# Moving one small product of a fused attention and feed-forward kernel ahead of group 6's turns

## The chip, the cores and the metric

The kernel runs on one core of one Trainium2 chip, as a single program. The metric is the device time of that program in microseconds (us). Five engines work side by side and wait for each other through semaphores: PE (matrix products; its weight loads are listed as PEld), DVE and ACT (vector and scalar work), POOL (here small copies and its own DMA queue) and SP (the queue from which most DMAs are issued).

## What is computed

The reference chains three stages on 1536 tokens (2 batches of 768), 8 heads of 64 columns. Cut to what matters here:

```python
k_sum = k.reshape(B, H, nb, 32, D).max(axis=3)      # nb = 24 blocks of 32 keys
v_sum = v.reshape(B, H, nb, 32, D).mean(axis=3)     # the "v means"
scores_l = scale * q @ k.T        # kept where |i - j| < 16
scores_s = scale * q @ k_sum.T + log(32)
a = softmax(concat[scores_l masked, scores_s])
attn = a @ concat[v, v_sum]
h = relu(x @ w_in); x = h * h @ w_out               # first feed-forward stage
out = silu(g) * val @ w_out2                        # second: RMS norm, gate and value products
```

## The kernel before, in words

Attention is done in 12 groups of 128 tokens, six for each batch: groups 0 to 5 are batch 0, groups 6 to 11 batch 1. For each group g the code has these steps, and the names are those of the rows below:

- `scores(g)`: PE writes the scores into two PSUM tiles, `s0` and `s1` (line 495).
- `softmax(g)`: DVE adds the mask (523) and takes the maximum `mx` (535; for some groups 541 and 542, with the subtraction on DVE). ACT takes the exponentials of `t`: eight small ACTIVATEs, one for each head (537), or one large one (543). DVE multiplies by the inverse sums, the norm (547).
- `ptrans(g)`, the group's "turns": PE turns `t` in two halves of four heads into `pps` (557), ACT copies each half to `pT` (560).
- `av(g)`: PE multiplies `pT` by `vx` into `xps` (581). `vx` holds, for each of four half-group slots, 96 rows of v (loaded by four DMAs of SP, line 475, the step `vload`) and the 24 rows of v means.
- `split_xs`: ACT casts `xps` to `xhi` (570), DVE forms the rest `xlo` (571). These are the input of the first feed-forward stage.

The rows of a large feed-forward product are laid between these steps: `h` = x times w_in (620) and `y` = the squared activation `hhi`, `hlo` times w_out (642), in passes of 256 tokens. Pass k needs the xhi and xlo of groups 2k and 2k+1: pass 3 (`h_3_0`, `h_3_2`) needs groups 6 and 7.

The v means of batch 1 are made apart from this. Seven accumulating DMAs of POOL add up `vsum` (409). `vs_mean(1)` multiplies it by a constant matrix into the PSUM tile `vmean` (414) and DVE copies that to `vm` (417). `vmput(0, 4)` lets POOL copy `vm` into the means' rows of all four slots of `vx` (462). av(6) is the first to read them.

Weights come as 64-bit words: SP loads them raw (`raw_wi`, line 188; `raw_wo`, line 192), and ACT and DVE turn them into numbers (203 to 224), in units that the loop slips between the other work.

A scheduler sets the final order on every engine: it takes the steps as the code writes them, plays them with its own estimates of duration, and lays each engine's instructions in the order in which they came out. `with after(...)` pins an instruction behind a marked one. Every engine then runs its list in order. The PSUM tiles of the attention steps are given out in turn from four buffers, in the order in which the code asks for them.

Of the kernel before, what the change touches and what calls it, by code (L numbers as in the profile page):

```python
# [32 lines left out]
def tile_window_attention_moe_moe2(  # L33
# [31 lines left out]
    GPB = S // P  # L65
    NG = NT // P
# [264 lines left out]
    def after(*marks):  # L331
        es = ExitStack()
        for m in marks:
            es.enter_context(tc.issue_after(mark[m].ins))
        return es
# [3 lines left out]
    def psA(name, shape=None):  # L339
        tag = rot["tags"][rot["i"] % len(rot["tags"])]  # L340
        rot["i"] += 1
        pool, bufs = {"a": (psB, 2), "h": (psB, 2), "y": (psY, MT // 2), "x": (psX, 2)}[tag]
        return pool.tile(shape or [P, 512], F32, tag=tag, name=name, bufs=bufs)
# [20 lines left out]
    def prep_begin(b):  # L364
        ksum = ap_.tile([P, NPAIR, NB], F32, tag="ksum", name=f"ksum{b}", bufs=1)
        state[b] = ksum

    def prep_load(b, c):
        state[("k", b, c)] = token_chunk(k, b, c, f"kr{b}_{c}")

    def prep_k(b, c):
        ksum = state[b]
        nb1 = 2 * P // QT
        kr = state.pop(("k", b, c))
        nb2 = 2 * P // BLK
        for hf in range(2):
            ps = psA(f"kps{b}_{c}_{hf}", [P, 2, 2 * P])
            for i in range(2):
                p = 2 * hf + i
                for j in range(2):  # L380
                    nc.tensor.transpose(
                        ps[:, i, j * P : (j + 1) * P], kr[:, j, p * P : (p + 1) * P], ident
                    )
            nc.vector.tensor_reduce(
                ksum[:, 2 * hf : 2 * hf + 2, nb2 * c : nb2 * (c + 1)],
                ps.rearrange("d p (n j) -> d p n j", j=BLK),
                axis=AX.X, op=ALU.max,
            )
            kv = kT[:, 2 * hf : 2 * hf + 2, WIN : WIN + NW1 * STEP].rearrange(
                "d p (n s) -> d p n s", s=STEP  # L390
            )[:, :, nb1 * c : nb1 * (c + 1)]
            pv = ps.rearrange("d p (n s) -> d p n s", s=QT)
            nc.scalar.copy(kv[:, :, :, 0:WIN], pv[:, :, :, 0:WIN])
            nc.scalar.copy(kv[:, :, :, WIN + NB : QT + NB], pv[:, :, :, WIN:QT])
# [11 lines left out]
    def vs_load(b):  # L406
        src = v[b].rearrange("h (p e) d -> p h e d", e=NE)
        for e in range(1, NE):
            mark["vs"] = nc.gpsimd.dma_start(vsum, src[:, :, e, :], accum_op=ALU.add)

    def vs_mean(b):
        ps = psA(f"vmean{b}", [K1, DM])[G0:K1]
        with after(("tr", GPB)):
            nc.tensor.matmul(ps, indv, vsum.rearrange("p h d -> p (h d)"), start=True, stop=True)
        vm = ap_.tile([K1, DM], F32, tag="vm", name=f"vm{b}", bufs=1)[G0:K1]
        state["vm"] = vm
        nc.vector.tensor_copy(vm, ps)
# [40 lines left out]
    def vrows(i0, n):  # L458
        return vx[G0:K1, i0 : i0 + n].rearrange("k i h d -> k i (h d)")

    def vmput(i0, n):
        nc.gpsimd.tensor_copy(vrows(i0, n), state["vm"].unsqueeze(1).to_broadcast([NB, n, DM]))
# [88 lines left out]
    def ptrans(g):  # L551
        t = state.pop(("t", g))
        pT = ap_.tile([NK, H, P], F32, tag="pT", name=f"pT{g}", bufs=2)
        for hf in range(2):
            ps = psA(f"pps{g}_{hf}")
            for j in range(4):
                mark[("tr", g)] = nc.tensor.transpose(  # L557
                    ps[0:NK, j * P : (j + 1) * P], t[:, 4 * hf + j, :], ident
                )
            mark[("pT", g)] = nc.scalar.copy(pT[:, 4 * hf : 4 * hf + 4, :], ps[0:NK].rearrange("n (h s) -> n h s", h=4))  # L560
        state[("pT", g)] = pT
# [11 lines left out]
    def av(g):  # L573
        pT = state.pop(("pT", g))
        ps = psA(f"xps1_{g}")
        for u in range(2):
            for p in range(NPAIR):
                o = p * P + QT * u
                for e in range(2):
                    with after(*((("s", 2),) if g == 1 else ())):  # L580
                        mark[("av", g)] = nc.tensor.matmul(  # L581
                            ps[QT * e : QT * e + QT, o : o + QT],
                            vx[:, (2 * g + u) % NVX, 2 * p + e, :],
                            pT[:, e * NPAIR + p, QT * u : QT * u + QT],
                            start=True, stop=True,
                        )
        split_xs(ps, g, 1)
        state["done"] = g
# [156 lines left out]
    def group(g):  # L745

        scores(g)
        if g > 3:
            vload(g)
        softmax(g)  # L750
        if g + 2 < NG and g % 2 == 0:
            qload(g + 2)
# [82 lines left out]
    def h_pair(k_, f):  # L835
        ps = psB.tile([P, CH], F32, tag="h", name=f"h0_{k_}_{f}", bufs=2)
        m = 2 * k_ % MT
        for j in range(2):
            units1.until(("wi", f + j))
            product(ps[:, G2 * j : G2 * (j + 1)], W[("wi", f + j)], xs[(1, 2 * k_ // MT)], m, m + 2)  # L840
        t = square(ps, f"0_{k_}_{f}")
        hq[(k_, f)] = hsplit(t, CH, f"0_{k_}_{f}")

    def y_pair(k_, f, between=()):
        if f == 0:
            for m in range(2):
                ys[m] = y_tile(k_, m, "y0_")
        hh = hq.pop((k_, f))
        for j in range(2):
            units1.until(("wo", f + j))  # L850
            ff_out(
                [ys[m] for m in range(2)], [t[:, G2 * j : G2 * (j + 1)] for t in hh],
                W[("wo", f + j)], f + j == 0, f + j == ROUNDS1[0] - 1,
            )
            if between:
                between[j]()
        if k_ == NK2 - 1:
            units1.used += 4
        if f == ROUNDS1[0] - 2:
            for m in range(2):  # L860
                gather(2 * k_ + m, ys.pop(m), 0, ROUNDS1, "y", None)
# [3 lines left out]
    for k_ in range(NK2):  # L865
        g, last = 2 * k_ + 3, 2 * k_ + 3 >= NG
        h_pair(k_, 0)
        if k_ == 0:
            av(2)
            group(4)  # L870
        if not last:
            ptrans(g)
        h_pair(k_, 2)
        if not last:
            av(g)
        if g == GPB - 1:
            group(GPB)
        if g + 2 < NG:
            group(g + 2)
            if k_ == 0:  # L880
                for c in range(NC2):
                    prep_load(1, c)
                vs_load(1)
        y_pair(k_, 0)
        if g + 1 < NG:
            ptrans(g + 1)
        if g + 1 == GPB:
            vs_mean(1)
            vmput(0, 4)
        if k_ == 0:  # L890
            prep_begin(1)
            prep_k(1, 0)
            y_pair(k_, 2, (lambda: prep_k(1, 1), lambda: prep_k(1, 2)))
            prep_kend(1, nc.vector, 0, NW1)
        else:
            if g + 3 < NG:
                qprep(g + 3)
            y_pair(k_, 2)
        if g + 1 < NG:
            av(g + 1)  # L900
        if k_ == 0:
            qprep(GPB)
        elif g + 3 < NG:
            group(g + 3)
        if k_ == 2:
            units1.cap = NW - 3
            units1.load(units1.cap)
            units1.lim = len(units1.units)
            units1.behind = (("exp", 9), ("norm", 9))
        if k_ == NK2 - 1:  # L910
            units1.behind = ()
        for _ in range(TICKS[k_]):
            units1.tick()
        if not last and g == NG - 1:
            actx.close()
            rot["tags"] = ("a",)
            side["cb"] = ctx.enter_context(
                tc.tile_pool(name="cbpool", bufs=1, side="right", reuse_waits="tile")
            )
            grow = side["cb"].tile([P, DM], F32, tag="grow", name="grow")  # L920
            side["pool"] = hand.enter_context(
                tc.tile_pool(name="w2pool", bufs=1, side="right", reuse_waits="tile")
            )
            side["psum"] = ctx.enter_context(
                tc.tile_pool(name="psY2", bufs=1, space=PSUM, reuse_waits="tile")
            )
            nc.sync.dma_start(grow, rms_g.partition_broadcast(P))
            units1.cap = NW + NRIGHT - 3
# [292 lines left out]
```

## Time and profile before

| | |
|---|---|
| median of 3 runs | 634.95 us (634.86 to 636.49) |
| the profiled execution | 636.93 us, its span 635.2 us |
| PE busy | 619.2 us, 97% of the span |
| DVE, ACT busy | 475.2 us (75%), 381.2 us (60%) |
| granted clock of PE, mean | 0.995 |

The profile follows one execution. Its times count from the start of the span; the 1.7 us between the span and the execution's time lie around it. Busy times say how full an engine is, the rows of waits say what an engine stood still for, and the timeline says when. The granted clock is 1.00 when PE runs at 2.4 GHz and 0.50 at 1.2 GHz. Group numbers are left out in the trace's rows, so that a row is told from its like by its time.

### The profile page before, as it was taken

The numbers are of one execution on the slowest core, as the hardware profiler recorded it, in microseconds if no ns is written. First come the engines' busy times: TensorE is split into PE (matmuls) and PEld (weight loads), VectorE is DVE, ScalarE is ACT, GpSimd is POOL, SyncE is SP. The second block draws the span as 40 slices with busy tenths as digits, with TensorE's granted clock in tenths as the row PEclk, the third lists the DMA queues.
The fourth block names the chain that finished last, engine by engine and source line by source line (L and its number), as shares of the span: only waits on it lengthen the run. The fifth ranks groups of instructions, "written<-read, shape, count | busy, mean of one in ns | idle before, by whom it ended". The sixth has DMA issues, their size and how long they took to land.

```text
span 635.2 us, 10103 instructions
## 1 busy us (share of the span) xinstructions
PE 619.2 (97%) x3794; PEld 522.5 (82%) x3794; DVE 475.2 (75%) x893; ACT 381.2 (60%) x823; POOL 54.6 (9%) x81
## 2 busy tenths in 40 slices
PE   8988998999999999999999999999999999999997
PEld 6576887888888888888888889889889888898886
DVE  4799776959996279987457869996977968976334
ACT  5795576757673257564443748867757567655252
POOL 4012110000000000000000000003112022022040
PEclk9998998999999999999999999999999999999999
DMA  9999913525333123220000005444734745535054
GB/s 245 287 209 211 179 29 84 179 54 166 99 101 99 34 66 101 71 96 0 1 1 1 2 0 199 134 133 68 173 97 83 179 91 95 147 46 87 1 85 115
DMA packets 85873, 64.23 MB, mean 101 GB/s; under 512 B 51904, under 2 KB 75456, under 8 KB 85824
## 3 DMA queue, kind: packets, MB, share of 16 engines
q1 hardware_dynamic: 74576, 51.72, 27.7%
q0 software_dynamic: 11248, 11.87, 13.0%
q8 instruction: 30, 0.49, 0.3%
q14 instruction: 19, 0.16, 0.1%
HBM read 49.94 MB, written 13.63 MB: 100 GB/s over the span
## 4 chain that ended last, share of the span: by engine, by line
PE 87%; DVE 7%; ACT 2%; DMA 1%; issue 1%; SPq 1%; DVEq 0%
PE y L642 20%; PE h L620 19%; PE z L642 15%; PE qa L1002 10%; PE qc L1002 5%; PE pa L1002 5%; PE pc L1002 3%; PE qb L1002 3%; PE s L495 1%; PE pps L557 1%; PE pb L1002 1%; PE xps L581 1%; PE xps L598 1%; DVE mx L531 1%; DMA kr<-in_k_dram 1%
## 5 line engine op out<-in xcount | busy, mean ns | idle before, releaser
L620 PE MATMUL h<-xhi,w_wi 128*128 128x512 f32 (+1 forms) x480 | 134.8, 354 | 4.6 <-ACT xhi L570 3.0
L642 PE MATMUL y<-w_wo,hhi 128*128 128x512 f32 x384 | 118.0, 393 | 1.6 <-DVE w_wo L224 0.8
L620 PEld LDWEIGHTS h<-xhi,w_wi 128*128 128x128 f32 x480 | 86.8, 194 | 17.9 <-ACT xhi L570 4.2
L620 PE MATMUL h<-xlo,w_wi 128*128 128x512 f32 (+1 forms) x240 | 85.0, 355 | 1.4 <-DVE xlo L571 1.4
L642 PEld LDWEIGHTS y<-w_wo,hhi 128*128 128x128 f32 x384 | 71.1, 188 | 16.8 <-DVE w_wo L224 1.2
L642 PE MATMUL z<-w_wp,hhiz 128*128 128x512 f32 x272 | 79.2, 390 | 0.0
L1037 POOL DMA_DIRECT2D out_dram<-zs x40 | 35.4, 1306 | 490.0 <-ACT zs L1033 490.0
L642 PE MATMUL y<-w_wo,hlo 128*128 128x512 f32 x192 | 72.8, 391 | 0.0
L642 PEld LDWEIGHTS z<-w_wp,hhiz 128*128 128x128 f32 x272 | 50.6, 188 | 10.2
L826 ACT ACTIVATE r<-h 128x512 f32<-128x512 f32 x48 | 28.8, 600 | 41.3 <-PE h L620 41.3
L620 PEld LDWEIGHTS h<-xlo,w_wi 128*128 128x128 f32 x240 | 46.7, 194 | 7.5 <-DVE xlo L571 2.1
L827 DVE TENSOR_TENSOR r<-h,r 128x512 f32<-128x512 f32 x48 | 32.9, 685 | 21.8 <-ACT r L826 21.8
L642 PE MATMUL z<-w_wp,hloz 128*128 128x512 f32 x136 | 48.1, 389 | 0.0
L631 ACT CAST hhi<-r 128x512 fp32r<-128x512 f32 x48 | 29.9, 622 | 25.9 <-DVE r L827 25.8
L642 PEld LDWEIGHTS y<-w_wo,hlo 128*128 128x128 f32 x192 | 35.9, 188 | 7.5 <-issue 0.2
L632 DVE TENSOR_TENSOR hlo<-r,hhi 128x512 fp32r<-128x512 f32 x48 | 33.8, 704 | 10.6 <-ACT hhi L631 10.3
L1033 ACT COPY zs<-z 128x512 f32<-128x512 f32 x48 | 25.6, 592 | 9.9 <-PE z L642 9.3
L642 PEld LDWEIGHTS z<-w_wp,hloz 128*128 128x128 f32 x136 | 25.5, 188 | 5.4
L1121 DVE TENSOR_TENSOR sg<-pb,sg 128x256 f32<-128x256 f32 x12 | 5.0, 423 | 25.3 <-PE pb L1002 25.3
L560 ACT COPY pT<-pps 120x512 f32<-120x512 f32 x24 | 13.9, 612 | 14.9 <-PE pps L557 14.8
L657 DVE TENSOR_TENSOR yp<-y,yp 128x512 f32<-128x512 f32 x24 | 15.6, 682 | 8.4 <-PE y L642 8.4
L537 ACT ACTIVATE t<-t,mx 128x120 f32<-128x120 f32 x48 | 18.3, 383 | 1.2 <-DVE mx L535 1.2
(246 smaller groups left out, 1327.1 us busy)
## 6 DMA issues: line engine op xcount, KB each, us to landing
out_dram<-zs POOLq DMA_DIRECT2D x40, 256.0 KB, 6.7
raw_wi<-in_moe_w_in_dram SPq DMA_DIRECT2D x16, 512.0 KB, 4.8
raw_wo<-in_moe_w_out_dram SPq DMA_DIRECT2D x16, 512.0 KB, 4.5
raw_wg<-in_moe_w_gate_dram SPq DMA_DIRECT2D x12, 512.0 KB, 3.7
raw_wv<-in_moe_w_val_dram SPq DMA_DIRECT2D x12, 512.0 KB, 4.6
raw_wp<-in_moe_w_out_dram SPq DMA_DIRECT2D x12, 512.0 KB, 3.3
kr<-in_k_dram SPq DMA_DIRECT2D x12, 256.0 KB, 4.4
qr<-in_q_dram SPq DMA_DIRECT2D x12, 256.0 KB, 4.7
```

Of the source, the lines that this page charges most:

```text
L537: mark[("exp", g)] = nc.scalar.activation(t[:, h], src[h], AF.Exp, bias=mx[:, h : h + 1], accum_out=sm[:, h : h + 1])
L560: mark[("pT", g)] = nc.scalar.copy(pT[:, 4 * hf : 4 * hf + 4, :], ps[0:NK].rearrange("n (h s) -> n h s", h=4))
L620: pe["last"] = nc.tensor.matmul(ps, a_, b_, start=(i == 0), stop=(i == tot - 1))
L631: nc.scalar.copy(hi[:, 0:n], s[:, 0:n]),
L632: nc.vector.tensor_tensor(lo[:, 0:n], s[:, 0:n], hi[:, 0:n].bitcast(F32), op=ALU.subtract),
L642: pe["last"] = nc.tensor.matmul(y, a_[:, ms], b_, start=(first and i == 0), stop=(last and i == 2))
L657: nc.vector.tensor_tensor(yp[g], ps, yp[g], op=ALU.add)
L826: nc.scalar.activation(t, ps, AF.Relu)
L827: nc.vector.tensor_tensor(t, ps, t, op=ALU.mult)
L1002: last = nc.tensor.matmul(ps, w[a_][:, kk], x[b_][:, kk], start=start and n == 0, stop=n == 3 * K2 - 1, skip_group_check=not start,)
L1033: nc.scalar.copy(s, ys.pop(m))
L1037: nc.gpsimd.dma_start(out[g * P : (g + 1) * P, :], s, accum_op=ALU.add)
```

## The change

The call of `vs_mean(1)` and `vmput(0, 4)` moves ahead of the turns of group 6, and the pin of its product is set to the scores of group 7 in place of the turns of group 6.

```diff
     def vs_mean(b):
         ps = psA(f"vmean{b}", [K1, DM])[G0:K1]
-        with after(("tr", GPB)):
+        with after(("s", GPB + 1)):
             nc.tensor.matmul(ps, indv, vsum.rearrange("p h d -> p (h d)"), start=True, stop=True)
...
         y_pair(k_, 0)
-        if g + 1 < NG:
-            ptrans(g + 1)
         if g + 1 == GPB:
             vs_mean(1)
             vmput(0, 4)
+        if g + 1 < NG:
+            ptrans(g + 1)
```

No instruction is added or left out, but the scheduler lays many in another order. On PE, the product stood between the turns of group 6 (`pps_0`, `pps_1`) and those of the next queries (`qps`). Before:

```order
L620 MATMUL h_2_2_1308<-xlo_1_948,w_wi_706 128x256
L557 MATMUL pps_0_1156<-ident,t_1082 120x128 x4
L557 MATMUL pps_1_1162<-ident,t_1082 120x128 x4
L414 MATMUL vmean_1168<-vsum,indv 24x512
L432 MATMUL qps_0_1174<-ident,qr_1099 128x128 x4
```

Now it stands in the middle of the first h product of pass 2:

```order
L620 MATMUL h_2_0_1263<-xlo_1_948,w_wi_578 128x256
L414 MATMUL vmean_1155<-vsum,indv 24x512
L620 MATMUL h_2_0_1263<-xhi_1_947,w_wi_578 128x256 x2
L620 MATMUL h_2_0_1263<-xlo_1_948,w_wi_578 128x256
L620 MATMUL h_2_0_1263<-xhi_1_947,w_wi_578 128x256
```

It moved ahead by 20 matmuls of h and the eight of group 6's turns. The second place is the end of pass 2 on PE, as the difference prints it in two pieces (`xps_6` and `xps_7` are av(6) and av(7), `s_8` and `s_9` scores, `pps_1_1302` the second half of group 7's turns, `pps_0_1408` and `pps_1_1414` the turns of group 8, `qps` the queries of groups 10 and 11):

```order
 L642 MATMUL y_2_1_1394<-w_wo_871,hhi_2_2_1336 128x512 x2
+L581 MATMUL xps_6_1202<-pT_1160,vx 64x64 x16
+L495 MATMUL s_8_1222<-kT,qT_1173 64x120 x8
+L581 MATMUL xps_7_1340<-pT_1295,vx 64x64
+L495 MATMUL s_9_1360<-kT,qT_1173 64x120 x8
 L642 MATMUL y_2_0_1393<-w_wo_871,hlo_2_2_1337 128x512
 L642 MATMUL y_2_1_1394<-w_wo_871,hlo_2_2_1337 128x512
```

```order
-L495 MATMUL s_9_1360<-kT,qT_1173 64x120 x8
 L557 MATMUL pps_1_1302<-ident,t_1124 120x128 x4
 L495 MATMUL s_9_1359<-kT,qT_1173 64x120 x8
 L581 MATMUL xps_7_1340<-pT_1295,vx 64x64 x15
+L557 MATMUL pps_0_1408<-ident,t_1243 120x128 x4
+L557 MATMUL pps_1_1414<-ident,t_1243 120x128 x4
+L432 MATMUL qps_0_1421<-ident,qr_1260 128x128 x4
 L620 MATMUL h_3_0_1515<-xhi_1_947,w_wi_555 128x256
```

av(6), half of the scores of groups 8 and 9 and the start of av(7) moved ahead of the last eight y matmuls, and the turns of group 8 moved ahead of pass 3. At the same place on ACT (`t_1243` is group 8, `t_1381` group 9, `pT_1295` group 7), before:

```order
L570 CAST xhi_1_947<-xps_6_1202 128x4x128
L560 COPY pT_1295<-pps_1_1302 120x512
L537 ACTIVATE t_1243,sm_1245<-t_1243,mx_1244 128x120 x8
L570 CAST xhi_1_947<-xps_7_1340 128x4x128
L543 ACTIVATE t_1381<-t_1381 128x960
```

and now, where the eight exponentials of group 8 stand ahead of the second half of group 7's pT, and group 7's xhi behind the exponential of group 9 and five conversions of weights:

```order
L570 CAST xhi_1_947<-xps_6_1202 128x4x128
L537 ACTIVATE t_1243,sm_1245<-t_1243,mx_1244 128x120 x8
L655 COPY yp_1447<-y_2_1_1394 128x512
L560 COPY pT_1295<-pps_1_1302 120x512
L543 ACTIVATE t_1381<-t_1381 128x960
L203 ACTIVATE x_wi_1712<-raw_wi_1509 128x512
L204 ACTIVATE u_wi_1713<-raw_wi_1509 128x512
L203 ACTIVATE x_wi_1846<-raw_wi_1511 128x512
L204 ACTIVATE u_wi_1847<-raw_wi_1511 128x512
L203 ACTIVATE x_wi_1857<-raw_wi_1513 128x512
L570 CAST xhi_1_947<-xps_7_1340 128x4x128
```

The third place is SP's queue behind vload(9); the four DMAs of `vx` that are kept in the middle are vload(10), which waits for av(8):

```order
-L192 DMA raw_wo_1975<-in_moe_w_out_dram 128x1024
-L188 DMA raw_wi_1977<-in_moe_w_in_dram 128x4x256
 L475 DMA vx<-in_v_dram 32x8x64
 L475 DMA vx<-in_v_dram 64x8x64
 L475 DMA vx<-in_v_dram 32x8x64
 L475 DMA vx<-in_v_dram 64x8x64
+L192 DMA raw_wo_1975<-in_moe_w_out_dram 128x1024
+L188 DMA raw_wi_1977<-in_moe_w_in_dram 128x4x256
```

The loads of two raw weights moved behind vload(10). On ACT, the first reader of that raw_wo (line 204, `u_wo_1985`) still stands ahead of pass 3's first relu, now with group 9's pT copies and group 10's exponentials behind that relu:

```order
L204 ACTIVATE u_wo_1985<-raw_wo_1975 128x512
L203 ACTIVATE x_wo_1984<-raw_wo_1975 128x512
L826 ACTIVATE r_3_0_1540<-h_3_0_1515 128x512
L560 COPY pT_1547<-pps_0_1548 120x512
L560 COPY pT_1547<-pps_1_1554 120x512
L204 ACTIVATE u_wi_1993<-raw_wi_1977 128x512
L537 ACTIVATE t_1492,sm_1494<-t_1492,mx_1493 128x120 x8
L631 CAST hhi_3_0_1543<-r_3_0_1540 128x512
```

Here the cast `hhi_3_0`, which the first y product of pass 3 reads, stands behind those eight exponentials; before, it stood ahead of them.

## Rows read from the trace of the kernel before

**Rows 1.** The page, busy us (share of the span) and instructions of PE.
```profile
PE 619.2 (97%) x3794; PEld 522.5 (82%) x3794; DVE 475.2 (75%) x893; ACT 381.2 (60%) x823; POOL 54.6 (9%) x81
```

**Rows 2.** Waits of PE from 80 to 330 us: total us, times, longest.
```profile
PE h L620 <- ACT xhi L570: 2.1, 1, 2.1
PE y L642 <- ACT hhi L631: 0.8, 1, 0.8
PE h L620 <- DVE xlo L571: 0.2, 1, 0.2
```

**Rows 3.** Timeline of PE: start us, duration, instruction, idle time before it.
```profile
85.74 0.40 PE L620 MATMUL h<-xhi,w_wi 128*128 128x256 f32 x2
...
89.10 1.04 PE L414 MATMUL vmean<-vsum,indv 96*24 96x512 f32 x2
...
97.11 0.62 PE L642 MATMUL y<-w_wo,hlo 128*128 128x512 f32 x2
...
99.02 1.15 PE L581 MATMUL xps<-pT,vx 120*64 120x64 f32 x32
...
103.85 1.15 PE L581 MATMUL xps<-pT,vx 120*64 120x64 f32 x30
107.12 0.60 PE L620 MATMUL h<-xhi,w_wi 128*128 128x256 f32 x2 [2.13 <-ACT xhi L570]
...
112.05 1.03 PE L557 MATMUL pps<-ident,t 128*120 128x128 f32 x8
...
116.24 1.15 PE L581 MATMUL xps<-pT,vx 120*64 120x64 f32 x30
```

**Rows 4.** Timeline of ACT around the first wait.
```profile
100.22 0.59 ACT L570 CAST xhi<-xps 128x512 fp32r<-128x512 f32 x1 [0.51 <-PE xps L581]
102.99 0.59 ACT L560 COPY pT<-pps 120x512 f32<-120x512 f32 x1 [2.18 <-PE pps L557]
103.47 0.40 ACT L537 ACTIVATE t<-t,mx 128x120 f32<-128x120 f32 x1
...
106.51 0.56 ACT L570 CAST xhi<-xps 128x512 fp32r<-128x512 f32 x1
107.10 1.01 ACT L543 ACTIVATE t<-t 128x960 f32<-128x960 f32 x1
...
110.28 0.66 ACT L203 ACTIVATE x_wi<-raw_wi 128x512 f32<-128x512 f32 x1
```

**Rows 5.** Windows: us, busy (count) of five engines, PE clock, DMA, GB/s.
```profile
108.50:110.80 2.30, 2.30 (x13) 2.30 (x12) 2.20 (x5) 2.30 (x5) 0.00 (x0) 0.50 0.62 227
...
126.00:127.00 1.00, 0.74 (x3) 0.65 (x4) 0.97 (x2) 1.00 (x3) 0.00 (x0) 1.00 1.04 378
```

**Rows 6.** Timeline of POOL: the last accumulating DMA, and the copy into vx.
```profile
75.97 1.31 POOL L409 DMA_DIRECT2D vsum<-in_v_dram  x1 [6.90 <-DMA vsum<-in_v_dram]
91.00 1.89 POOL L462 COPY vx<-vm 24x2048 f32<-24x2048 f32 x1 [13.71 <-DVE vm L417]
```

**Rows 7.** DMA issues from 75.9 and from 120.0: KB, us to landing.
```profile
vsum<-in_v_dram POOLq DMA_DIRECT2D x1, 192.0 KB, 4.3
...
raw_wo<-in_moe_w_out_dram SPq DMA_DIRECT2D x1, 512.0 KB, 4.4
```

**Rows 8.** Timeline of DVE around the first wait.
```profile
102.13 1.15 DVE L535 TENSOR_REDUCE mx<-t 128x8 f32<-128x960 f32 x1
...
105.85 1.16 DVE L542 TENSOR_TENSOR t<-t,mx 128x960 f32<-128x960 f32 x1
...
107.79 1.15 DVE L547 TENSOR_TENSOR t<-t,sm 128x960 f32<-128x960 f32 x1
```

**Rows 9.** Timeline of SP's queue: when DMAs were issued.
```profile
107.00 0.61 SPq L192 DMA_DIRECT2D raw_wo<-in_moe_w_out_dram  x1
...
116.95 2.96 SPq L475 DMA_DIRECT2D vx<-in_v_dram  x4
120.02 0.56 SPq L192 DMA_DIRECT2D raw_wo<-in_moe_w_out_dram  x1
```

## The prediction

> **What bounds the kernel now.** The page comes first. PE is busy for 619.2 of 635.2 us, the next engine, DVE, for 475.2 [rows 1], so I ask at what PE stands still. The groups of waits answer that for the stretch which the change touches: between 80 and 330 us PE waits three times, 2.1 us for group 7's xhi, 0.8 us for the first hhi of pass 3 and 0.2 us for group 7's xlo [rows 2], and I found no wait of PE from 330 us on until the last microsecond. Nothing behind these waits has slack to take a delay in: what PE loses near 110 us arrives at the end in full, and what it wins there is won. So the sum is one over PE's idle time and PE's clock between 85 and 130 us, before and after.
>
> Before, that stretch loses four things. PE has finished av(7) at 105.0 (103.85 and 1.15), its h product starts at 107.12 after a wait of 2.13 [rows 3]. ACT cast that xhi only at 106.51, when group 8's eight exponentials (103.47 to 106.51, so 3.04) were through [rows 4]. Then 0.21 for xlo. In the h product that follows the granted clock is 0.50, that is 1.2 GHz, while after the wait of 0.80 it stays 1.00 [rows 5]. What the slow clock cost: two h matmuls started 0.24 apart at 2.4 GHz, since the 3.36 us from 85.74 to 89.10 hold 20 of them and the turns, eight of them taking about 0.95 net of overlap [rows 3], so 0.12 each; the 25 between 107.12 and 112.05 should take 3.0 and took 4.93, of which 0.21 is the wait for xlo. About 1.7 is lost. With the last 0.80 the stretch loses 2.13 + 0.21 + 1.7 + 0.80 = 4.85.
>
> **The change part by part.** *The moved product* is one entry of 1.04 [rows 3] wherever it stands, so PE's work up to the last scores of group 9 is the same and ends at 103.85 as before. It moves ahead by that 3.36 us, to 85.74. Its operand is there: the last accumulating DMA was issued at 75.97 [rows 6] and lands 4.3 later [rows 7], at 80.3. POOL's copy into vx began 1.90 after the product (91.00 less 89.10) and takes 1.89 [rows 3, 6], so it now ends at 89.5, long before av(6). Cost on PE: nothing; if the cover were gone, av(6) would be late by the overlap, and there are 7 us of it.
>
> *av(6) earlier.* Since vx is ready, av(6) goes ahead of the last eight y matmuls, to 97.11 instead of 99.02 [rows 3]. Group 8's scores and maximum come 1.9 earlier, and here the order on ACT turns round. mx of group 8 was done at 103.28 [rows 8], 4.26 behind the start of av(6); now at 101.4. Its exponentials run from 101.4 to 104.4, and group 7's second pT, which stood ahead of them, stands behind, with a yp copy between. At 0.48 a step (102.99 to 103.47 [rows 4]) and 0.59 for its own length, pT is ready at 104.4 + 0.48 + 0.59 = 105.5. PE is at the rest of av(7) at 103.85. **Wait a: 1.65.** Bounds: nothing if the yp copy and pT found ACT free, which the order excludes, and 2.1 if mx comes 0.5 later because y's rows lie between the scores.
>
> *Group 8's turns ahead of pass 3.* av(7) then ends at 106.65. Next on PE stand group 8's turns, which need DVE's norm. DVE's subtraction for group 9 still starts at 105.85 for 1.16, since it hangs on scores that end when they did; the norm (1.15) follows the small sums [rows 8]: 107.0 + 0.3 + 1.15 = 108.5. **Wait b: 1.85** (1.2 if the norm stands ahead of the subtraction's end by half of it, 2.5 if xlo still comes between, 0.65).
>
> *Group 7's xhi far back on ACT.* Turns and half of the queries take PE to about 109.9 (1.03 for eight and half of that, less overlap). xhi now stands behind the exponential of group 9, which cannot start before 107.0, and five conversions; these ended at 110.94 (110.28 and 0.66) [rows 4]. xhi starts as they overlap, at 110.85, and PE's product starts 0.61 behind such a start, as at 106.51 and 107.12: 111.45. **Wait c: 1.55** (1.2 to 2.1). av(8) then needs two pT copies that stand behind xhi: **wait d: 0.5**, from 0.3 to 0.7. Together 1.65 + 1.85 + 1.55 + 0.5 = 5.55, where 2.34 stood.
>
> *The clock there.* The rows show the drop behind 2.13 and none behind 0.80 [rows 5]. Three waits of 1.55 to 1.85 with 1.2 to 1.4 of work between lie nearer to the former; I take one drop of the size of before, 1.6, with bounds of 0 and 3.5 (two). Speaking to this, the Trainium skill (TensorE: Matmul & The Clock Gate, "HAM oscillation — how this bites in real kernels") says that bursts of matmuls set between waits go back to the slow clock and that each starts cold. By that rule this stretch would lose some 3 instead of 1.6. The 2.13 agrees with it, the 0.80 does not.
>
> *The raw weights behind vload(10).* The raw_wo was issued at 107.00 and is now behind four vx DMAs. Those wait for av(8): 116.95 against its start at 116.24, and they take 2.96; the next raw_wo left at 120.02 [rows 9], so 3.78 behind av(8)'s start [rows 3]. With the waits above av(8) starts at about 113.0, raw_wo leaves at 116.8 and lands 4.4 later [rows 7], at 121.2. On ACT, queued behind its first reader: two conversions, pass 3's relu, group 9's two pT, one conversion, the exponentials of group 10, then hhi. At 0.57 a conversion ((110.94 - 107.10 - 1.01) / 5 [rows 4]) pT are ready near 123.3 and 123.9, and hhi at 123.9 + 0.57 + 3.04 + 0.6 = 128.1. PE meanwhile has av(8) and scores (2.7, half of the 5.98 less the turns in 99.02 to 105.0), 48 h matmuls at 0.12, the turns, all in all 9.4, and with the slow clock 10: it stands at group 9's av at 123.0. **Wait e: 0.8** over both halves. Then av(9) and group 11's scores end near 125.8 and the y product waits for hhi to 128.2: **wait f: 2.4**, where 0.80 stood. xhi of group 9 and hlo come just behind, 0.7. Place B: 3.9, bounds 0.3 (raw_wo is there anyway) and 5.8 (it takes 6.3 to land). As f is above 2.13, I add 1.1 for the clock (0 to 1.7).
>
> *The sum.* 5.55 + 1.6 + 3.9 + 1.1 - 4.85 = **+7.3**. The profiled span of 635.2 becomes 642.5, and its execution, 636.93 with 1.7 around the span, 644.2. That execution is 2.0 above the median of the runs, 634.95, on which I put the sum: **642.3**.
>
> **The rivals.** *Only place A.* If raw_wo is issued by about 113.5 it lands before ACT asks for it; place B then costs 0.3 instead of 3.9 and 1.1, though still under 0.8: 5.55 + 1.6 + 0.3 - 4.85 = +2.6, with the 0.8 kept +3.1: about 638.0. For it: SP was ahead at 107.00 [rows 9]. Against it: the order puts the vx DMAs ahead, and 2.96 us of issue lie between.
>
> *More.* Two drops of the clock at A, or a raw_wo that takes 6 us: +11, about 646 and above.
>
> *No difference.* The clock stays full through the short waits and B is hidden: 5.55 + 0.8 - 4.85 = +1.5: 636.5. The 0.80 with clock 1.00 speaks for it, the nearness of 1.85 to 2.13 against.
>
> *Faster.* av(6) is earlier by 1.9, and if that let ACT reach group 7's xhi earlier by as much as PE, the wait of 2.13, the 0.21 and the slow clock would go: -4.0, 630.9. That is decided by ACT reaching xhi by 106.2. It has 3.84 us between the exponential of group 9 and that cast [rows 4], none of which stood ahead of xhi before; 4.7 would have to vanish.
>
> **How the numbers follow.** Two places: 0.60. Only A: 0.19. More: 0.08. No difference: 0.08. Faster: 0.05. What a measurement can tell from no change is 0.3%, 1.9 us. So faster 0.05, same 0.08, slower 0.87. The forecast is 642.3; the range leaves out the faster, most of the no difference and the upper half of more: 637.3 to 646.0. The likeliest case alone is 640.0 to 645.0.
>
> **What the profile after would show.** The product at about 85.7 with no wait, and av(6) near 97.1. PE waiting for ACT's pT at 103.85, for DVE's norm near 106.7 and for xhi near 110, each 1.2 to 2.1. A granted clock of 0.50 in some of 104 to 115. SP issuing raw_wo at 116 to 118, ACT idle for it until about 121, and a wait of y for hhi over 2 us. From 135 us on no new waits, and rows as before but 7 us later. I am wrong if PE's order lets other rows fill a to d, if ACT is not idle at 121 (then only A), or if further waits appear after 135, where I have put nothing.

## The result and the profile after

The changed kernel takes 643.01 us (median of 6 runs, 641.48 to 644.56), the kernel before 636.02 (6 runs, 634.86 to 637.07): a ratio of 1.0107, 95% interval 1.0092 to 1.0123. It is slower by 7.0 us, where the forecast was 7.3. The execution profiled of it is its fastest one: 641.48, span 639.7, only 4.5 over the span of before, whose profiled execution (636.93) lies 0.9 above the median of its kernel. A second execution of the changed kernel, profiled later, has a span of 641.9. Both are read below, since they differ in an instructive way. In what follows place A is the stretch from av(6) to the start of pass 3's h product (some 97 to 113 us), place B the end of pass 3's h products and the first y product behind them (some 116 to 130).

The waits of PE from 80 to 330 us in the first execution answer to [rows 2]:

```profile
PE y L642 <- ACT hhi L631: 2.0, 1, 2.0
PE xps L581 <- ACT pT L560: 1.7, 1, 1.7
PE pps L557 <- DVE t L547: 0.9, 1, 0.9
PE y L642 <- DVE hlo L632: 0.4, 1, 0.4
PE h L620 <- ACT xhi L570: 0.2, 1, 0.2
```

Together they make 5.25 where 3.14 stood, and there is none from 330 us on: as forecast, whatever is lost here arrives at the end. The timeline of PE in the same execution shows where, beside [rows 3]:

```profile
85.16 1.04 PE L414 MATMUL vmean<-vsum,indv 96*24 96x512 f32 x2
...
96.61 1.15 PE L581 MATMUL xps<-pT,vx 120*64 120x64 f32 x32
...
105.10 1.97 PE L581 MATMUL xps<-pT,vx 120*64 120x64 f32 x30 [1.70 <-ACT pT L560]
107.94 1.93 PE L557 MATMUL pps<-ident,t 128*120 128x128 f32 x8 [0.87 <-DVE t L547]
109.66 1.06 PE L432 MATMUL qps<-ident,qr 128*128 128x128 f32 x4
110.92 0.80 PE L620 MATMUL h<-xhi,w_wi 128*128 128x256 f32 x2 [0.20 <-ACT xhi L570]
...
112.58 1.15 PE L581 MATMUL xps<-pT,vx 120*64 120x64 f32 x30
113.66 1.05 PE L495 MATMUL s<-kT,qT 64*64 64x120 f32 x32
...
121.22 0.83 PE L495 MATMUL s<-kT,qT 64*64 64x120 f32 x10
...
126.70 1.20 PE L642 MATMUL y<-w_wo,hhi 128*128 128x512 f32 x4 [2.05 <-ACT hhi L631]
```

The product and av(6) run without a wait and some 0.5 ahead of the forecast, since this execution reached the place earlier. Then the forecast waits come in their order: for the second half of pT, for the norm, for xhi. Two groups are long for their kind: av(7) takes 1.97 where av(8) takes 1.15, and the eight turns 1.93 where 1.03 was read before [rows 3]. That is the clock, which stands at 0.50 for the whole of this window of the first execution, across the waits for the norm and for xhi:

```profile
105.50:111.50 6.00, 4.94 (x42) 4.30 (x39) 5.86 (x11) 4.92 (x9) 0.00 (x0) 0.50 0.29 66
```

ACT, with what held it up, beside [rows 4]:

```profile
100.96 0.40 ACT L537 ACTIVATE t<-t,mx 128x120 f32<-128x120 f32 x1 [2.57 <-DVE mx L535]
...
104.00 0.56 ACT L655 COPY yp<-y 128x512 f32<-128x512 f32 x1
104.47 0.58 ACT L560 COPY pT<-pps 120x512 f32<-120x512 f32 x1
...
110.29 0.58 ACT L570 CAST xhi<-xps 128x512 fp32r<-128x512 f32 x1
...
119.89 0.66 ACT L204 ACTIVATE u_wo<-raw_wo 128x512 int32<-128x512 uint32 x1 [3.15 <-DMA raw_wo<-in_moe_w_out_dram]
...
126.05 0.60 ACT L631 CAST hhi<-r 128x512 fp32r<-128x512 f32 x1
```

Group 8's exponentials hold pT until 104.47, xhi stands at 110.29 behind five conversions, and at 119.89 ACT has stood still for 3.15 us for the raw_wo, with hhi behind it at 126.05. The load's issue on SP, beside [rows 9], where it left at 107.00:

```profile
97.33 18.22 SPq L475 DMA_DIRECT2D vx<-in_v_dram  x12
115.60 0.61 SPq L192 DMA_DIRECT2D raw_wo<-in_moe_w_out_dram  x1
```

The second execution of the same kernel, PE and then the reader of raw_wo on ACT:

```profile
105.19 1.97 PE L581 MATMUL xps<-pT,vx 120*64 120x64 f32 x30 [1.70 <-ACT pT L560]
...
123.34 0.33 PE L581 MATMUL xps<-pT,vx 120*64 120x64 f32 x2 [1.22 <-ACT pT L560]
...
127.93 1.19 PE L642 MATMUL y<-w_wo,hhi 128*128 128x512 f32 x4 [2.07 <-ACT hhi L631]
```
```profile
121.12 0.67 ACT L204 ACTIVATE u_wo<-raw_wo 128x512 int32<-128x512 uint32 x1 [4.30 <-DMA raw_wo<-in_moe_w_out_dram]
```

The load left at the same time (115.69) and came 1.2 later, and PE waits 1.22 for group 9's pT, which the first execution did not. The windows from 100 to 140 us, as in [rows 5], of the kernel before, of the first execution and of the second:

```profile
100.00:120.00 20.00, 17.66 (x224) 15.83 (x221) 18.80 (x33) 14.86 (x37) 0.00 (x0) 0.91 0.40 104
120.00:140.00 20.00, 19.20 (x195) 16.48 (x194) 14.18 (x24) 15.01 (x49) 0.00 (x0) 1.00 0.47 147
```
```profile
100.00:120.00 20.00, 17.23 (x185) 15.20 (x186) 18.60 (x31) 12.34 (x33) 0.00 (x0) 0.83 0.35 92
120.00:140.00 20.00, 17.43 (x173) 14.20 (x173) 11.79 (x21) 14.69 (x48) 0.00 (x0) 1.00 0.47 147
```
```profile
100.00:120.00 20.00, 17.23 (x186) 15.19 (x185) 18.60 (x31) 12.21 (x32) 0.00 (x0) 0.83 0.33 84
120.00:140.00 20.00, 16.71 (x139) 13.29 (x137) 11.19 (x20) 13.11 (x45) 0.00 (x0) 0.91 0.50 157
```

From 100 to 120 us, around A, the granted clock is 0.83 in both against 0.91 before; from 120 to 140, around B, it is 1.00 in the first and 0.91 in the second. The later load and this lower clock are the distance between the two executions: the second is 0.1 behind the first at av(8) (112.67 and 112.58) and 2.2 behind it in its span. The median of the runs, 643.0, lies above the first one's 641.5.

### The profile page after: what moved, and what is told of

Read it like the earlier page. It is cut to its first block, busy times and chain, and to the rows that moved or that the text cites. A ratio compares the mean times of both kernels' runs of the same rounds, so it can differ in the third digit from the quotient of the medians.

```text
span 639.7 us, 10100 instructions
## 1 busy us (share of the span) xinstructions
PE 623.8 (98%) x3794; PEld 527.3 (82%) x3794; DVE 476.2 (74%) x893; ACT 381.5 (60%) x823; POOL 54.6 (9%) x81
## 4 chain that ended last, share of the span: by engine, by line
PE 90%; DVE 3%; DMA 3%; ACT 2%; SPq 1%; issue 0%; ACTq 0%; DVEq 0%
PE y L642 21%; PE h L620 20%; PE z L642 15%; PE qa L1002 10%; PE qc L1002 5%; PE pa L1002 5%; PE pc L1002 3%; PE qb L1002 3%; PE s L495 2%; PE xps L581 2%; DMA qr<-in_q_dram 2%; PE pps L557 1%; PE pb L1002 1%; PE qps L432 1%; PE xps L598 1%; DMA raw_wo<-in_moe_w_out_dram 1%
## 5 line engine op out<-in xcount | busy, mean ns | idle before, releaser
L620 PE MATMUL h<-xhi,w_wi 128*128 128x512 f32 (+1 forms) x480 | 133.3, 352 | 0.2 <-ACT xhi L570 0.2
L581 PEld LDWEIGHTS xps<-pT,vx 120*64 120x64 f32 x384 | 15.2, 152 | 6.3 <-ACT pT L560 2.8
```

The lines of the kernel that those rows point to most:

```text
L581: mark[("av", g)] = nc.tensor.matmul(ps[QT * e : QT * e + QT, o : o + QT], vx[:, (2 * g + u) % NVX, 2 * p + e, :], pT[:, e * NPAIR + p, QT ...
L620: pe["last"] = nc.tensor.matmul(ps, a_, b_, start=(i == 0), stop=(i == tot - 1))
```

## The experiments

My theory was that the order which the scheduler made of the change costs the time: at A through ACT (a copy or cast that stands behind eight exponentials), at B through SP and ACT (the late raw_wo). The rivals were PE's own work, the product itself with its buffers, and a loss elsewhere. All ratios are against the kernel before, run beside the kernel in question; they are estimated from all runs of both and can differ by up to 0.001 from the quotient of the two medians.

**pairs**: PE's rows alone.

```diff
-                    with after(*((("av", 1),) if g == 3 else ())):
+                    with after(*({3: (("av", 1),), 11: (("av", 9),)}.get(g, ()))):
```

> Only PE's order changes: the scores of group 11 all stand behind av(9) and alternate between their two tiles, where the changed kernel issues them in blocks of one tile (its group 11 took some 2.1 us of PE, that of before 1.2). If the y product of pass 3 is held up by hhi on ACT (theory: the order on ACT and SP sets the time at place B), PE only waits longer, 2.9 in place of 2.05, and the time stays that of the changed kernel, 1.0107 of before within 0.002. If PE's own extra work is what costs (rival), 0.9 us come back: 642.1, ratio 1.009.

Measured 643.56, ratio 1.0108 (1.0093 to 1.0123): no change. Its waits of PE:

```profile
PE xps L581 <- ACT pT L560: 3.9, 3, 2.0
PE pps L557 <- DVE t L547: 1.7, 1, 1.7
PE y L642 <- ACT hhi L631: 1.1, 1, 1.1
```

The 0.9 of work that was to leave PE came back as waits for ACT, for group 9's pT (2.0) and for hhi (1.1; the expectation had put all of it there, as 2.9). Behind the first of them the scores ran at the lower clock in the profiled execution. At B the changed kernel hangs on ACT, and blocks of scores only fill a wait. The wait for the norm is 1.7 here: in this execution av(7) ran in 1.15.

**wo4_late**: the late load no longer stands ahead of ACT's other work.

```diff
     FIRST = {
+        (1, 11): [("exp", 10)],
```

> The conversions of the late raw_wo are pinned behind the exponentials of group 10, so pass 3's relu, group 9's pT, those exponentials and hhi no longer stand behind that load; the load itself leaves as late as in the changed kernel. Theory (the load blocks ACT): PE's wait for hhi falls from 2.05 to 0.8 or less, hlo's 0.43 with it, the y product of pass 3 starts about 2.5 us earlier against the scores before it, and the time falls by 2.0 to 2.8 against the changed kernel: about 640.5, ratio 1.007. Rival (place B is hidden or paid elsewhere): within 0.7 us of the changed kernel, ratio 1.010 to 1.011.

Measured 639.18, ratio 1.0047 (1.0031 to 1.0062): 3.8 us less than the changed kernel, more than the 2.0 to 2.8 expected. The expectation had left out what the second execution shows, a wait of 1.22 for pT and a slow clock at B. It had also left out that the order on PE changes: the scores of group 11 alternate again and take 1.3 in place of 2.1. How much each of these adds is not parted. Its windows:

```profile
104.00:116.00 12.00, 9.96 (x113) 8.36 (x113) 11.66 (x23) 8.14 (x15) 0.00 (x0) 0.57 0.23 53
120.00:132.00 12.00, 12.00 (x130) 10.59 (x129) 8.31 (x15) 10.51 (x38) 0.00 (x0) 1.00 0.65 199
```

PE is busy for all of 120 to 132: place B is gone, and place A stands alone, with waits of 1.71, 1.69 and 0.19 and a granted clock of 0.57. So the changed kernel's loss parts into some 3.1 us at A (639.18 less 636.10, the median of before beside it) and some 3.8 at B. By the intervals of the ratios the first lies between 2.0 and 3.9 and the second is no better known than to some 1.4.

**xhi_first**: group 7's xhi ahead of the five conversions.

```diff
-            units1.behind = (("exp", 9), ("norm", 9))
+            units1.behind = (("exp", 9), ("norm", 9), ("xhi", 7, 1))
```

> The five conversions of weights are pinned behind group 7's xhi, so that cast stands right behind the exponential of group 9 on ACT; the order at place B changes with it (hhi of pass 3 now ahead of the late raw_wo's conversions and of group 10's exponentials). Theory: place A keeps its waits for pT (1.7) and for the norm (0.9) and its slow clock, since xhi was waited for only 0.2; place B loses its 2.05 and 0.43. Time 2 to 3 below the changed kernel: 640 to 641, ratio 1.006 to 1.008. Rival (xhi is what place A hangs on, as the prediction's wait c of 1.55 had it): the waits at A shrink too and 3.5 to 5 come back: 638 to 639.5.

Measured 640.86, ratio 1.0078 (1.0053 to 1.0104), as the theory had it, and the waits agree: those for pT (1.70) and the norm (1.69) at A are still there and none for xhi, so A does not hang on xhi; at B hhi is waited for no more, but group 9's pT, now behind the load, for 2.00.

**exp8_late**: group 8 is called behind group 7's turns.

```diff
         if not last:
             ptrans(g)
+        if k_ == 2:
+            group(8)
...
-        elif g + 3 < NG:
+        elif g + 3 < NG and k_ != 1:
             group(g + 3)
```

> The scores and softmax of group 8 are called behind group 7's turns; the v means' product stays where the changed kernel has it. On ACT group 7's second pT and its xhi now stand ahead of group 8's exponentials, and half of group 9's scores stand between av(7) and the h product of pass 3. Theory (the changed kernel loses through ACT's order): no wait of PE over 1.2 between 97 and 115, no granted clock of 0.50 there, and hhi of pass 3 not behind the late load; then even what before loses there (2.13, 0.21 and 1.7 of slow clock) is mostly gone: 632 to 634.5, ratio 0.994 to 0.998. Rival (the earlier product itself, or the traffic it brings, costs): slower than before, 638 or more.

Measured 638.48, ratio 1.0039 (1.0024 to 1.0054). The rival's range holds it, but not for the rival's reason. Place A has no wait over 0.5 and a granted clock of 1.00, as the theory said. The loss moved to B, a wait for group 9's xhi:

```profile
104.00:116.00 12.00, 11.50 (x137) 10.45 (x136) 11.71 (x22) 11.21 (x31) 0.00 (x0) 1.00 0.15 34
```
```profile
127.91 0.79 PE L620 MATMUL h<-xhi,w_wi 128*128 128x256 f32 x2 [3.75 <-ACT xhi L570]
```

I had read the load's place on ACT against hhi and not against group 9's xhi, which stands behind it (ACT waits 1.58 for the load here) and behind group 10's exponentials.

**both_xhi9** and **both_xhi9_b**: exp8_late with the load's conversions behind group 9's xhi, on the changed kernel and on the one before.

```diff
+        (1, 11): [("xhi", 9, 1)],
```

> Group 8 behind group 7's turns as in exp8_late, and the late raw_wo's conversions pinned behind group 9's xhi. In exp8_late place A had no wait of PE over 0.5, and PE lost 3.7 in one wait for group 9's xhi, which stood on ACT behind the conversions of that load and group 10's exponentials held up with them, and ran at a granted clock of 0.50 behind it. Theory (what is left in exp8_late is the late load on ACT): that wait falls to 1 or less, the slow clock behind it goes, 4 to 6 us less than exp8_late's 638.5: 632.5 to 634.5, ratio 0.994 to 0.998, faster than both kernels. Rival (another wait takes its place): 637 or more.

> The same two edits on the kernel before, so that the v means' product stands where it stood before; against both_xhi9 this takes back the change under study and nothing else. Theory (the product itself is worth nothing, only what the order does with it): within 1 us of both_xhi9, ratio within 0.0016 of it. Rival (the earlier product and av(6) ahead of eight y matmuls are worth their 1.9): 1.5 to 2 us slower than both_xhi9.

Measured 637.40, ratio 1.0011 (0.9998 to 1.0024), and 636.46, ratio 1.0008 (0.9992 to 1.0023). The first fell to the rival: the wait for xhi9 shrank from 3.75 to 1.70, since eight exponentials still stand ahead of that cast, and the clock falls behind it. It is the loss of the kernel before [rows 2], one pass later, and it stands in both kernels alike (both_xhi9 first):

```profile
127.18 0.50 PE L621 MATMUL h<-xhi,w_wi 128*128 128x256 f32 x2 [1.70 <-ACT xhi L571]
```
```profile
126.31 0.51 PE L621 MATMUL h<-xhi,w_wi 128*128 128x256 f32 x2 [1.67 <-ACT xhi L571]
```

The pair answers the question of the study: with the product moved or not, in an order otherwise nearly the same, no difference can be told. The ratios lie 0.0003 apart, each known to some 0.0015; the medians lie 0.9 us apart, and not on the side that the rival's 1.5 to 2 us had put down.

**tile_only**: the kernel before, only the PSUM tile taken earlier.

```diff
+        if g + 1 == GPB:
+            state["vsps"] = psA("vmean1", [K1, DM])
         if g + 1 < NG:
             ptrans(g + 1)
```

> The kernel before with only the PSUM tile of the product taken ahead of group 6's turns, as the changed kernel takes it: all engines' orders are those of before, and four attention tiles stand in other buffers. Theory (order, not buffers): the time of before, ratio 0.998 to 1.002. Rival (the exchanged buffers hold something up): part of the 7 us, ratio 1.003 or more.

Measured 636.82, ratio 1.0002 (0.9990 to 1.0014). All orders are those of before; the exchanged buffers cost nothing that 12 runs can tell.

**after_again**: the changed kernel, for the second profile shown above.

> The changed kernel once more, for a second profile: the first one's execution was the fastest of six and 1.5 below their median. Theory (the slow clock falls otherwise in each execution and trades against the waits): 642 to 644.5; wait for pT 1.70 again, the wait for the norm between 0.87 and 1.7, and where the clock is lower the waits behind it are shorter. Rival (something outside places A and B differs): waits or slow clock after 135 us.

643.67. The wait for the norm was 0.86, as in the first, and no new wait stands behind 135 us.

**g10_s** and **x_s89**: both_xhi9 with pins on the scores (x_s89: the first diff line; g10_s: the second, with group 10 called behind av(9), and with the last four exponentials of groups 8 and 10 pinned behind the xhi of the group before, which the expectation does not name; in its profile that cast stands ahead of all eight).

```diff
+                    with after(*({3: (("av", 1),), 8: (("av", 6),), 9: (("av", 7),), 11: (("av", 9),)}.get(g, ()))):
...
+                    with after(*({3: (("av", 1),), 8: (("av", 6),), 9: (("av", 7),), 10: (("av", 9),), 11: (("xlo", 9, 1),)}.get(g, ()))):
```

> both_xhi9 with group 10's scores and softmax called behind av(9), as group 8's behind group 7's turns, and with the scores of groups 8 to 11 pinned so that those of 9 and 10 alternate between their tiles and stand between an av and the next h product. So neither xhi7 nor xhi9 stands behind exponentials on ACT, and scores or y matmuls cover both casts on PE. Theory (what before, both_xhi9 and the changed kernel lose here is one thing, a cast of xhi or a pT behind eight exponentials, and the slow clock that such a wait brings): no wait of PE over 0.6 from 97 to 135, granted clock 1.00 there, 3.5 to 5 us less than before: 631.5 to 633, ratio 0.992 to 0.995. Rival (the waits move on, as from exp8_late to both_xhi9): 635 or more.

> both_xhi9 with only the pins on the scores of groups 8, 9 and 11: those of 9 and 11 alternate between their tiles (0.98 a group in place of 1.94), which takes 1.9 of work off PE; xhi9 still stands behind group 10's exponentials. Theory (PE's own work counts only where it does not wait behind): place A gives its 0.97, at the wait for xhi9 (1.70 in both_xhi9) the saving turns into waiting: 636 to 637, ratio 0.999 to 1.001. Rival (PE's work is the bound here too): 634.5 to 635.5, ratio 0.997 to 0.998.

g10_s took 638.62, ratio 1.0038 (1.0025 to 1.0051), the rival: the load now leaves only at 123.26, group 10's exponentials wait behind it, and PE waits 1.79 for their norm and 1.74 for pT at 135 to 138. x_s89 took 633.89, ratio 0.9957 (0.9943 to 0.9972), faster than both kernels and below both expected ranges. Its windows:

```profile
104.00:116.00 12.00, 11.24 (x133) 9.99 (x133) 11.51 (x22) 10.86 (x30) 0.00 (x0) 1.00 0.15 34
120.00:132.00 12.00, 10.81 (x127) 9.98 (x126) 11.32 (x20) 10.77 (x42) 0.00 (x0) 1.00 0.88 293
```

The granted clock is 1.00 in both windows, and the longest wait is 0.84. The expectation had two things wrong. The pins take some 1.4 of work off PE and not 1.9, since group 11's scores took 1.5 in both_xhi9 already, not 1.94. And in the order that the pins gave, group 9's xhi stands ahead of group 10's exponentials on ACT, not behind. On PE the scores of groups 9 and 11 stand between an av and the next product, and cover the casts. So this run does not part the saved work from the removed wait; b_s89 below shows what saved work is worth where the waits stay.

**x_s89_b** and **b_s89**: the same on the kernel before, and there only the pins on groups 8 and 9.

```diff
+                    with after(*({3: (("av", 1),), 8: (("av", 6),), 9: (("av", 7),)}.get(g, ()))):
```

> x_s89 (the fastest so far, 0.9957) on the kernel before: the v means' product and av(6) stand where they stood before, all else as in x_s89. Theory (the place of the product is worth nothing by itself): 633.2 to 634.6, ratio 0.995 to 0.9975. Rival (in an order without long waits the earlier av(6) is worth its 1.9): 635.5 or more, ratio 0.999 or more.

> The kernel before with only the pins on the scores of groups 8 and 9, which take 1.9 of work off PE; group 8's exponentials still stand ahead of group 7's xhi, and the pins move the late raw_wo behind vload(10), as in the changed kernel. Theory (work counts only where nothing is waited for): the gain is lost again in the wait for xhi7 and at place B: 635.5 to 640, ratio 0.999 or more. Rival (PE's work is the bound): 633.5 to 635, ratio 0.996 to 0.998.

x_s89_b: 633.20, ratio 0.9959 (0.9945 to 0.9973): the place of the product is again worth nothing that the runs can tell. b_s89: 638.74, ratio 1.0045 (1.0032 to 1.0058): the scores of groups 8 and 9 take 1.9 less of PE (those of group 11 0.4 more), and the kernel is slower, with waits for xhi7 and xhi9:

```profile
105.27 0.50 PE L620 MATMUL h<-xhi,w_wi 128*128 128x256 f32 x2 [2.51 <-ACT xhi L570]
...
128.43 0.50 PE L620 MATMUL h<-xhi,w_wi 128*128 128x256 f32 x2 [1.52 <-ACT xhi L570]
```

Where such waits stand, PE's own work is not what bounds the stretch. How the gain of x_s89 divides between the waits removed and the work saved stays open.

## Why the prediction was right

- **The product costs nothing, and is worth nothing.** Right: no wait for it, av(6) earlier by what was forecast, and two pairs of kernels (both_xhi9, x_s89) that differ in its place and not, beyond the noise, in time.
- **The waits at A.** Wait a, 1.65, measured 1.70 or 1.71 in all five profiled executions with that order. Wait b, 1.85, measured 1.69 where av(7) ran at full clock, and 0.87 and 0.86 where it ran slow. Wait c, 1.55, measured at most 0.20, and d, 0.5, nothing over 0.15. The step that failed is "The clock there", added to the waits as a term of its own. At 1.2 GHz the turns took 1.93 and half of the queries 1.06, so that PE came to xhi when it was nearly there: one stretch of time was counted as a wait and as a slow clock. The ends of the waits show it. The forecast has them at 105.5, 108.5 and 111.45, the first execution at 105.10, 107.94 and 110.92, each 0.4 to 0.6 earlier, and av(6) was 0.5 earlier already. So ACT and DVE let PE go when the forecast said they would, and what PE lost to the clock before these moments it would otherwise have waited: in pairs, where av(7) ran at full clock, the norm came as long after pT as in the changed kernel (2.83 and 2.84). The slow clock itself was undersized: av(7) lost 0.8, the turns 0.9, and the queries and matmuls up to 112.58 over 1, some 3 in place of 1.6. Waits and clock together come to some 5.9 up to av(8) (1.70, 0.87, 0.20, 0.1 and 3), where 5.55 and 1.6 make 7.15.
- **The raw weights.** Right in mechanism and nearly in size: issue at 115.60 (forecast 116.8), a wait for hhi of 2.05 and 2.07 (2.4), hlo 0.43 in the first execution (0.7), the wait for pT 1.22 in the second execution and 0.09 in the first (0.8), the clock at B lower in one of two (1.1). Taken back it gives 3.8, where 5.0 was forecast.
- **The rivals.** Only A: refuted by wo4_late. No difference, faster and more: refuted by the time. The slow clock at A was as large as "more" had it, but it lay inside the waits.
- **Not foreseen.** Group 11's scores, in blocks of one tile, took 2.1 of PE in place of 1.2. They lay inside the waits of B, as pairs showed, and cost nothing there.

That 7.3 came so near to 7.0 is in part luck. By the medians A costs 3.1 net where 5.55 + 1.6 - 4.85 = 2.3 was forecast, B 3.8 where 5.0 was, and neither is known to better than about 1 us. The single executions scatter as widely: the spans of the two profiled ones are 4.5 and 6.7 above that of before, and what A costs hangs on how long the clock stays low. In the execution of wo4_late it stays there until 116, so that av(8) and the scores behind it take 1.97 and 1.88 in place of 1.15 and 1.05.

The rule that was weighed, from the Trainium skill (TensorE: Matmul & The Clock Gate, "HAM oscillation — how this bites in real kernels"), is told there of a kernel with longer waits, for DMA, each of which sends the next burst back to the slow clock. At A some 3 us were lost, which is what the prediction gave as the sum by that rule, but not burst by burst: the clock is at 0.50 through 105.50 to 111.50 with two waits inside, one drop, as I had taken it, only longer than that of before, where 0.50 is read from 108.50 to 110.80 [rows 5] and 1.00 again from 111.0. At B the drop does not come each time: behind the 2.05 of the first execution the granted clock is 1.00.

What stays open is why the clock falls behind the first wait in some executions (both of the changed kernel) and around the second in others (pairs, wo4_late, xhi_first), and why it stays low for longer in some. The runs show that it does, and that the wait behind it shrinks by as much: 0.82 more for av(7) and 0.82 less for the norm.

## What to carry to other kernels

On an engine that is busy 97% of the time, ask of a moved instruction not what it costs but which list it re-sorts: here one product of 1.04 us cost nothing that could be told at either place, and the 7 us came from casts and copies that the scheduler laid behind eight exponentials or behind a late load on another engine. Do not add a slow clock to a wait that follows it in the same stretch; in these traces what the one took the other gave. And when a wait is removed, look up who stands next behind the same exponentials or the same load: three of these kernels only moved the wait on, and the order that won has the casts ahead of the exponentials, other work of PE in front of their readers, and some 1.4 us less of scores.

## What was not expected of the hardware

Scores of one group take half the time when the two tiles alternate. Two rows of the kernel before, a block of one tile and a whole group in turn:

```profile
100.10 1.04 PE L495 MATMUL s<-kT,qT 64*64 64x120 f32 x16
...
117.32 1.05 PE L495 MATMUL s<-kT,qT 64*64 64x120 f32 x32
```

Sixteen matmuls of 64 rows take 1.04 when they write one tile, and thirty-two take 1.05 when they write two in turn, each tile from its own 64 rows. Both stand at a granted clock of 1.00.

Between 85 and 330 us, single waits of 0.58 and 0.84 (x_s89) and 0.80 (before) left that clock at 1.00. Behind waits of 1.52 to 3.75 for xhi in front of an h product it fell each time (b_s89, both_xhi9 and both_xhi9_b, before, exp8_late), within the wait or up to 1.6 us behind it, and in front of the y product it stayed at 1.00 behind 2.05 and fell behind 2.07 (the two executions of the changed kernel).
